# Sequence DFT with rows paired to their mirror, in batches 2 to 7 of a fused FNet and ELU kernel

## The chip, the cores and the metric

The kernel runs on one core of a Trainium2 chip, as one launch. The metric is device time in microseconds, the median of the runs. Five engines work side by side: TensorE (PE; matmuls and, overlapping them, weight loads), VectorE (DVE), ScalarE (ACT), GpSimd (POOL) and SyncE (SP), whose queue issues most of the DMA transfers. Each engine works through its instructions in the order in which they stand in the program, and waits where an operand isn't ready.

## The reference

```python
# x: (8, 3008, 256) float32, w_in: (256, 2048), w_out: (2048, 256)
X = np.fft.fft(x, axis=1)
X = np.fft.fft(X, axis=2)
y = X.real.astype(np.float32).reshape(8 * 3008, 256)
h = y @ w_in
g = np.where(h > 0.0, h, np.exp(np.minimum(h, 0.0)) - 1.0)
out = (g @ w_out).astype(np.float32)
```

So each batch gets a DFT along its sequence of 3008 rows and one along its 256 channels, of which the real part is kept, and then a two-layer network with ELU is applied to every row.

## The kernel before

**Folding.** The channel DFT is folded into the first weight matrix (`Wc` for the cosine part, `Ws` for the sine part), so at run time only the sequence DFT is computed. The input is real, so output rows k and 3008 - k come from the same two numbers, the cosine part R and the sine part I: h for row k is P + Q, for row 3008 - k it is P - Q. Only 1504 columns a batch are therefore needed, 12032 in all, in 47 tiles of 256 columns.

**The sequence DFT of a batch.** Four quarters of x, loaded as `xl0` to `xl3` (two of them backwards, by gathers with row tables `ix` from GpSimd's queue, L181; two forwards from SP, L197 and L198), are added and subtracted on GpSimd (`fold_x`, L527) to four sets of rows: even and odd in the channel direction (E for R, O for I), and for even and odd k (`kodd` 0 and 1). Each set has 6 blocks of 128 rows. A DFT unit (`Dft`, one for each of R and I and each `kodd`) has two halves, one for even and one for odd rows of the sequence. Each half is three matmuls against columns of a matrix `MC` (L430, in `dft_mms`); `dft_parts` gives block, first column, width and place in the PSUM bank. The even half is then unfolded: a copy on ScalarE (`anti`) and a sum and a difference on VectorE (L436) give `es`. The odd half is joined with it by `plus` and `minus`, one sum and one difference on VectorE (L436), into a ring of 2048 columns in SBUF (`Rr` for R, `Ir` for I), forwards and backwards. Where a run crosses the end of the ring, it is cut in two.

**The steps.** The rest is a sequence of 376 steps, eight for each tile of 256 columns, each for two blocks of 128 of d_ff. A step's matmuls: P (`H<-Rr,Wc`), Q (`H<-Ir,Ws`) and, from step 16 on, seven products against the second weight matrix in a form with 7 products in place of 8 (`mm_X1`, `mm_X2`, `mm_X3`, into `pA` to `pD`), which belong to the step before last. Between P and Q VectorE makes E (L839), which reads P and must be done before Q adds to the same bank. VectorE then makes the difference for row 3008 - k (L853) and both ELUs (L869), with ScalarE's `Relu` and `Exp` (L442). GpSimd makes four sums of G for the seven products (`sum_1`, `sum_3`, `sum_2`, `sum_4`, L439). At the end of a tile VectorE combines the four accumulators (u, v) and transposes them (L1017, L1038) into `ot`, of which there are two, and SP stores `ot`. In the first step of a tile, number 0, `mm_X3` is put off by most of a step, so that step number 2 has two matmuls fewer and number 3 two more.

**The order.** The order is written out by hand: `at(t, fn)` puts each piece of work at a time in units of the step period, and at the end all pieces are issued in the order of these times. Instructions of PE, DVE, ACT and POOL are pinned to this order; most DMAs of SP are placed by the framework. A batch b of 1 to 7 is computed while the tiles of batch b - 1 run: with s0 = 47 (b - 1) its loads stand from step s0 - 8 on, its folds from s0 - 1 to s0 + 38, and its four DFT units (R and I of kodd 0, then R and I of kodd 1) have their even halves at the ends of steps s0 + 28, 34, 38 and 42 and their odd halves two steps later. The unfold, and plus and minus, stand in the following step on VectorE, after E. In this text "step 2" and the like is the step's number within its tile of eight; since 47 is one short of a multiple of 8, it moves by one from batch to batch.

In the last batch one backward row does not exist, so a special table column is used for one gather and a plain transfer from GpSimd's queue (L192) puts the right row over it.

Of the kernel before, what the change touches and what calls it, by code (L numbers as in the profile page):

```python
# [9 lines left out]
FP = mybir.dt.float32  # L10
BF = mybir.dt.bfloat16
U32 = mybir.dt.uint32
# [15 lines left out]
NH = 189  # L28
BE = 4 * NH
BW = BE + 3 * NE  # L30
GW = 7 * TW
PERIOD = 4.8


def _dft_consts():

    p = np.arange(128)[:, None]
    out = np.zeros((128, 4, BW), np.float64)
    for ri in range(2):
        fn = np.cos if ri == 0 else np.sin
        for kodd in range(2):
            mat = out[:, 2 * ri + kodd]
            n, h = (NO, NO // 2) if kodd else (NE, NH)

            def block(m, n):  # L50
                k = 2 * np.arange(n)[None, :] + kodd
                s = 4 * p + m if m < 4 else 508 + 2 * p + m
                w = np.where(s == 0, 0.5, 1.0) * (s <= RUN)
                w = np.where(s == RUN, 0.5 if ri == kodd else 0.0, w)
                return s, w * fn(2.0 * np.pi * ((s * k) % SEQ) / SEQ)

            for m in (0, 2, 4):
                s, v = block(m, h)
                anti = (s % 4 == 2) != ri
                if not kodd:  # L60
                    v[:, h - 1] *= ~anti[:, 0]
                if m < 4:
                    c = 0 if m == 2 * ri else h
                    mat[:, c : c + h] = v
                else:
                    mat[:, 2 * h : 3 * h] = v * ~anti
                    mat[:, 3 * h : 4 * h] = v * anti
            for t in range(3):
                mat[:, BE + t * NE : BE + t * NE + n] = block(2 * t + 1, n)[1]
    return out.reshape(128, -1).astype(np.float32)  # L70


def _chan_consts():
# [33 lines left out]
def kernel(  # L107
# [11 lines left out]
    n_tiles = (n_cols + TW - 1) // TW  # L119

    MC_dr = nc.inline_tensor(_dft_consts(), name="dft_mats")
    CC_dr = nc.inline_tensor(_chan_consts(), name="chan_mats")
    PK_dr = nc.inline_tensor(_pick_consts(), name="pick_mats")

# [14 lines left out]
    def xrows(b, row, step, n, rows=6):  # L139

        return bass.AP(
            tensor=xt,
            offset=x.offset + (b * SEQ + row) * ND,
            ap=[[step * ND, n], [1, rows * ND]],
        )


    xflat = x.rearrange("b s d -> (b s) d")
    ix = cpool.tile([128, 3], I32, tag="ix")

    def row_tables():

# [17 lines left out]
    def load_x(b):  # L170

        L = [
            spool.tile([128, 6 * ND], FP, tag=f"xl{j}", bufs=1, name=f"xl{j}")
            for j in range(4)
        ]

        def back(j, few):
            cols = slice(0, 2 * ND) if few else slice(2 * ND, 6 * ND)
            c = 1 if few else 2 if j == 1 and b == NB - 1 else 0
            pin(  # L180
                nc.gpsimd.indirect_dma_start(  # L181
                    out=L[j][:, cols],
                    out_offset=None,
                    in_=xflat,
                    in_offset=bass.IndirectOffsetOnAxis(
                        ap=ix[:, c : c + 1].bitcast(U32), axis=0
                    ),
                    element_offset=(b * SEQ + (HALF if j == 1 else 0)) * ND,
                )
            )  # L190
            if b == NB - 1 and j == 1 and not few:
                nc.gpsimd.dma_start(  # L192
                    out=L[1][0:1, 2 * ND : 5 * ND], in_=xrows(b, SEQ - 3, 1, 1, 3)
                )

        def ahead(j, row):
            nc.sync.dma_start(out=L[j][:, 0 : 4 * ND], in_=xrows(b, row, 4, 128, 4))  # L197
            nc.sync.dma_start(  # L198
                out=L[j][:, 4 * ND :], in_=xrows(b, row + 512, 2, 128, 2)
            )  # L200

        loads = [lambda n=n: back(2 - n // 2, n % 2) for n in range(4)]
        return L, loads + [lambda: ahead(3, HALF), lambda: ahead(0, 0)]


    CC = cpool.tile([128, 384], FP, tag="CC")
# [191 lines left out]
    def load_mats(ri, kodd, cuts=()):  # L398
        n = (2 * ri + kodd) * BW
        ends = (0, *cuts, BW)  # L400
        for a, z in zip(ends, ends[1:]):
            nc.sync.dma_start(
                out=MC[ri, kodd][:, a:z], in_=MC_dr.ap()[:, n + a : n + z]
            )

    warm = cpool.tile([128, 1], FP, tag="warm")
    nc.vector.memset(warm, 0.0)
    Rr = cpool.tile([128, RING], FP, tag="Rr")
# [32 lines left out]
    def act(o, i, func=AF.Copy, **kw):  # L441
        pin(nc.scalar.activation(out=o, in_=i, func=func, **kw))  # L442
# [75 lines left out]
        gtt(W[3], W[1], b21, ALU.add)  # L518


    def fold_x(L, engine_of, cuts_of):

        ops = {}

        def op(key, o, a, b, f):
            tt = lambda o, a, b, f: pin(
                engine_of(key).tensor_tensor(out=o, in0=a, in1=b, op=f)  # L527
            )
            cuts = cuts_of(key, o.shape[1])
            for i in range(len(cuts) - 1):  # L530
                c = slice(cuts[i], cuts[i + 1])
                ops[key, i] = lambda c=c: tt(o[:, c], a[:, c], b[:, c], f)

        E, O = [], []
        for j in range(4):
            e = spool.tile([128, 6 * 128], FP, tag=f"e{j}", bufs=1, name=f"e{j}")
            o = spool.tile([128, 6 * 128], FP, tag=f"o{j}", bufs=1, name=f"o{j}")
            ev, ov = (
                t.rearrange("p (m o d) -> p m o d", o=2, d=64) for t in (e, o)
            )  # L540
            src = L[j].rearrange("p (m d) -> p m d", d=ND)
            if j in (1, 2):
                src = src[:, ::-1]

            lo, hi = (
                t.rearrange("p m (d o) -> p m o d", o=2)
                for t in (src[:, :, 1:129], src[:, :, 255:127:-1])
            )
            op(f"e{j}", ev, lo[:, :, ::-1], hi[:, :, ::-1], ALU.add)
            ops[f"c{j}", 0] = lambda e=ev[:, :, 0, 63:64], s=src[:, :, 0:1], j=j: (  # L550
                act(e, s)
                if engine_of("c") is nc.vector and j != 1
                else pin(engine_of("c").tensor_copy(out=e, in_=s))
            )
            op(f"o{j}", ov, lo, hi, ALU.subtract)
            E.append(e)
            O.append(o)
        ops["x1", 0] = lambda: act(L[1][0:1, 5 * ND :], L[0][0:1, 0:ND])
        op("E0", E[0], E[0], E[1], ALU.add)
        op("E2", E[2], E[2], E[3], ALU.add)  # L560
        op("EO0", E[1], E[0], E[2], ALU.add)
        op("EO1", E[3], E[0], E[2], ALU.subtract)
        op("O0", O[0], O[0], O[1], ALU.subtract)
        op("O2", O[2], O[2], O[3], ALU.subtract)
        op("EO2", O[1], O[0], O[2], ALU.subtract)
        op("EO3", O[3], O[0], O[2], ALU.add)
        return [E[1], E[3], O[1], O[3]], ops

    FOLDS = (
        "e0 c0 e3 c3 e2 c2 x1 e1 c1 E0 E2 EO0 o0 o3 o2 o1 O0 O2 EO2 EO1 EO3".split()  # L570
    )

    def fold_first(L):
# [57 lines left out]
    class Dft:  # L631
# [42 lines left out]
        def half(self):  # L674

            if self.ri == 0 and not self.kodd:
                R4b = R4[:, self.b : self.b + 1]
                vtt(R4b, self.es[:, 0:1], self.odd[:, 0:1], ALU.subtract)


    def load_ext(j, s0, s1):
        if j == 0 and s0 == 0:
# [495 lines left out]
        w2_chunks[5].load()  # L1178

    def open_x(b):  # L1180
        state["L"], state["loads"] = load_x(b)

    def begin_x_even():
        state["x_even"] = Dft(0, 0, 0, fold_first(L_first), ring=Rb, first=True)
# [219 lines left out]
    def at_dft(step, gap, b, ri, kodd, stat):  # L1404
        box = []

        def d():
            if not box:
                box.append(Dft(ri, b, kodd, stat()))
            return box[0]  # L1410

        at_half(step, d, 0, 0)
        at_half(step + gap, d, 1, b * HALF + (kodd + 1) * RUN)

    def begin_folds(b):
        state["EO"], state["ops"] = fold_x(
            state["L"], lambda key: nc.gpsimd, lambda key, n: (0, n // 2, n)
        )

    steps_b = HALF * 8 // TW  # L1420
# [20 lines left out]
    at(35 * T + 4.76, lambda: ext_side(3))  # L1441
    at(36 * T + 0.2, lambda: ext_unfold(1, vtt))
    at(36 * T + 1.5, lambda: ext_rows(1, vtt))
    fold_keys = [(k, p) for k in FOLDS for p in range(2 if k[0] not in "cx" else 1)]
    n_big = sum(k[0] not in "cx" for k, _ in fold_keys)
    for b in range(1, NB):
        s0 = (b - 1) * steps_b
        late = 2 if b == 1 else 0
        l0, gap = (s0 - 8, 1) if b > 1 else (3.2, 0.5)
        if b > 1:  # L1450
            at(l0 * T + 0.1, lambda b=b: open_x(b))
        for n in range(6):
            t = l0 + gap * n if n < 4 else l0
            if b > 1:
                at(t * T + 0.2, lambda n=n: state["loads"][n]())
        first = (6, 7, 7, 8, 9, 9, 10, 10, 12, 15)

        def fold_slot(n):
            if b > 1:
                return s0 - 1 + 39 * n // n_big  # L1460
            return first[n] if n < len(first) else 17 + n - len(first)
# [3 lines left out]
        for key in fold_keys:  # L1465
            slot = fold_slot(n)
            at(
                slot * T + (3.5 if slot < 16 else 1.3),
                lambda key=key: state["ops"][key](),
            )  # L1470
            n += key[0][0] not in "cx"
        for n, (ri, kodd) in enumerate(((0, 0), (1, 0), (0, 1), (1, 1))):
            at_dft(
                s0 + (28, 34 + late, 38 + late, 42 + late)[n], 2, b, ri, kodd,
# [54 lines left out]
```

## Time and profile before

| | us |
|---|---|
| median of 3 runs | 1945.42 |
| lowest and highest | 1945.23, 1945.55 |
| span of the profiled execution | 1943.2 |
| steps 16 to 375, from first P to last P | 121.63 to 1925.40 |

| busy, from the page and its groups | us | count |
|---|---|---|
| GpSimd, sums of G (L439) | 1036.8 | 1440 |
| VectorE, E (L839) | 327.7 | 752 |
| VectorE, difference and both ELUs | 256.8, 255.8, 256.7 | 376 each |
| GpSimd, first folds of x (L527, 128x384) | 66.6 and 66.0 | 56 and 56 |
| GpSimd, folds of folds | 56.2 and 56.1 | 56 and 56 |
| GpSimd, gathers (L181) | 32.5 | 32 |

A row of the groups gives line, engine and operation, then output and inputs by their names in the program, shapes, count, busy time and the mean of one, and the idle time just ahead of it. In the timelines a line holds start, duration over all the merged instructions, engine, line, operation, names, shape and count, and in brackets the idle time of the engine just ahead of it and who ended it. The recorded duration of a matmul reaches beyond the start of the next one, since matmuls are pipelined.

### The profile page before, as it was taken

How to read it: one execution, taken by the hardware profiler on the slowest of the kernel's cores; microseconds unless marked ns; L12 is line 12 of the kernel's file. 1: busy time of each engine (PE TensorE's matmuls, PEld its weight loads, DVE VectorE, ACT ScalarE, POOL GpSimd, SP SyncE). 2: the span in 40 equal slices, each digit the busy share in tenths (PEclk: the TensorE clock that was granted, in tenths of full speed). 3: DMA queues.
4: the chain of work that ended last, by engine and by line, in shares of the span. 5: the costliest groups of instructions: out<-in, count | busy, mean ns of one | idle time of the engine just before them, and what ended most of it. 6: DMA issues, size and time to landing. Idle time of an engine off the chain costs nothing.

```text
span 1943.2 us, 26993 instructions
## 1 busy us (share of the span) xinstructions
PE 1933.4 (99%) x8912; PEld 1653.4 (85%) x8912; DVE 1293.2 (67%) x2398; ACT 865.6 (45%) x1671; POOL 1377.6 (71%) x1816
## 2 busy tenths in 40 slices
PE   9999999999999999999999999999999999999999
PEld 6788788888888888888888888888888888888887
DVE  8866666666666666666667666676666766667666
ACT  5644434443444444444444443444434444344443
POOL 4788758876677767787677876777767776556655
PEclk9999999999999999999999999999999999999999
DMA  8145111101112020020210202012020110100101
GB/s 333 44 35 52 34 44 19 49 15 33 33 20 49 12 50 21 18 50 11 54 23 13 52 8 58 12 20 60 7 52 11 20 23 14 17 12 11 23 11 23
DMA packets 263291, 70.25 MB, mean 36 GB/s; under 512 B 248607, under 2 KB 249523, under 8 KB 263153
## 3 DMA queue, kind: packets, MB, share of 16 engines
q1 hardware_dynamic: 257360, 55.69, 14.8%
q0 software_dynamic: 3616, 12.59, 2.1%
q8 instruction: 70, 1.15, 0.2%
q14 instruction: 69, 0.56, 0.1%
q10 hardware_dynamic: 2176, 0.26, 0.1%
HBM read 43.66 MB, written 24.80 MB: 35 GB/s over the span
## 4 chain that ended last, share of the span: by engine, by line
PE 94%; DVE 2%; POOL 2%; ACT 1%; DMA 1%; issue 1%; DVEq 0%; POOLq 0%
PE H L430 38%; PE pB L430 16%; PE pC L430 16%; PE pD L430 16%; PE pA L430 8%; DMA xl<-in_x_dram,ix 1%; POOL WT L439 1%; POOL G L439 1%; DVE G L869 0%; DVE E L839 0%; DVE e L527 0%; POOL w L439 0%; DVE v L436 0%; ACT G L442 0%; DVE pow L310 0%
## 5 line engine op out<-in xcount | busy, mean ns | idle before, releaser
L439 POOL TENSOR_TENSOR G<-G 128x256 f32<-128x256 f32 x1440 | 1036.8, 730 | 508.5 <-DVE G L869 338.6
L839 DVE SCALAR_TENSOR_TENSOR E<-Rb,wex,H 128x256 f32<-128x256 f32 x752 | 327.7, 477 | 544.7 <-PE H L430 541.1
L442 ACT ACTIVATE G<-H 128x512 f32<-128x512 f32 x376 | 224.6, 597 | 960.1 <-DVE G L853 955.4
L430 PE MATMUL H<-Ir,Ws 128*128 128x256 f32 x1504 | 386.9, 380 | 2.0 <-DVE E L839 2.0
L430 PE MATMUL H<-Rr,Wc 128*128 128x256 f32 x1504 | 387.0, 380 | 0.8 <-DVE Ir L436 0.8
L430 PE MATMUL pC<-G,WT 128*128 128x256 f32 x1440 | 369.5, 379 | 0.0
L430 PEld LDWEIGHTS H<-Rr,Wc 128*128 128x128 f32 x1504 | 284.6, 190 | 56.0 <-issue 2.2
L430 PEld LDWEIGHTS H<-Ir,Ws 128*128 128x128 f32 x1504 | 278.8, 189 | 49.6 <-DVE E L839 4.3
L430 PEld LDWEIGHTS pC<-G,WT 128*128 128x128 f32 x1440 | 273.6, 190 | 37.2
L853 DVE SCALAR_TENSOR_TENSOR G<-E,H 128x512 f32<-128x512 f32 x376 | 256.8, 683 | 44.2 <-POOL G L439 5.0
L869 DVE SCALAR_TENSOR_TENSOR G<-G,H 128x512 f32<-128x512 f32 x376 | 255.8, 680 | 43.0 <-ACT G L442 43.0
L869 DVE SCALAR_TENSOR_TENSOR G<-M,G 128x512 f32<-128x512 f32 x376 | 256.7, 683 | 0.4 <-ACT M L442 0.4
L442 ACT ACTIVATE G<-G 128x512 f32<-128x512 f32 x376 | 233.2, 620 | 0.0
L430 PE MATMUL pD<-G,w 128*128 128x256 f32 x784 | 229.4, 379 | 0.5 <-POOL G L439 0.5
L430 PE MATMUL pA<-G,w 128*128 128x256 f32 x784 | 229.3, 379 | 0.0
L430 PE MATMUL pB<-G,w 128*128 128x256 f32 x784 | 229.3, 379 | 0.0
L442 ACT ACTIVATE M<-G 128x512 f32<-128x512 f32 x376 | 224.0, 596 | 3.1 <-DVE G L853 3.1
L442 ACT ACTIVATE M<-M 128x512 f32<-128x512 f32 x376 | 221.0, 588 | 0.1
L430 PE MATMUL pB<-G,WT 128*128 128x256 f32 x720 | 214.8, 380 | 0.3
L430 PE MATMUL pD<-G,WT 128*128 128x256 f32 x720 | 214.1, 379 | 0.0
L430 PEld LDWEIGHTS pD<-G,w 128*128 128x128 f32 x784 | 148.9, 190 | 21.1 <-POOL G L439 0.9
L430 PEld LDWEIGHTS pA<-G,w 128*128 128x128 f32 x784 | 149.0, 190 | 20.5
(148 smaller groups left out, 1408.2 us busy)
## 6 DMA issues: line engine op xcount, KB each, us to landing
out_dram<-ot SPq DMA_DIRECT2D x496, 32.0 KB
xl<-in_x_dram SPq DMA_DIRECT2D x16, 512.0 KB
xl<-in_x_dram SPq DMA_DIRECT2D x16, 256.0 KB
out_dram<-ot SPq DMA_DIRECT2D x256, 2.0 KB
Rb<-r SPq DMA_DIRECT2D x10, 376.0 KB
raw<-in_moe_w_in_dram SPq DMA_DIRECT2D x7, 512.0 KB
MC<-dft_mats SPq DMA_DIRECT2D x3, 943.5 KB
raw<-in_moe_w_out_dram SPq DMA_DIRECT2D x4, 512.0 KB
```

The lines of the kernel that those rows point to most:

```text
L430: nc.tensor.matmul(out_, lhsT=lhsT, rhs=rhs, start=start, stop=stop, skip_group_check=True)
L439: pin(nc.gpsimd.tensor_tensor(out=o, in0=a, in1=b, op=op))
L442: pin(nc.scalar.activation(out=o, in_=i, func=func, **kw))
L839: nc.vector.scalar_tensor_tensor(out=S.E[:, c], in0=Rb[:, cols(i)], scalar=wex[:, f : f + 1], in1=S.H[:, c], op0=ALU.mult, op1=ALU.add,)
L853: nc.vector.scalar_tensor_tensor(out=two(S.G[:, 0:512])[:, :, ::-1], in0=two(S.E), scalar=2.0, in1=two(S.H), op0=ALU.mult, op1=ALU.subtract,)
L869: nc.vector.scalar_tensor_tensor(out=o, in0=e, scalar=-1.0, in1=h, op0=ALU.add, op1=ALU.max)
```

## The change

For batches 2 to 7 the rows of a quarter are no longer put in 6 blocks by their distance modulo 4 or 2, but in three pairs of blocks in which each row of a multiple of 8 has its mirror at a distance 4 modulo 8 in the same place (`_row_pairs`). Blocks 0, 2 and 4 hold even rows, 1, 3 and 5 odd ones. The even half then splits once more: parts a (rows of multiples of 8), b (4 modulo 8) and c (2 modulo 4) are computed for a quarter or half of the k alone and unfolded twice, near (a and b) and far (with c). For `kodd` 0 the odd half splits too: sums and differences of blocks 1 and 3 (S and D) are formed on GpSimd and multiplied with half the columns each. In `kodd` 1 the odd half keeps its width.

The new matrices (1417 columns for kodd 0, 1786 for kodd 1) are loaded into the buffers of the old ones at steps 52, 55, 58 and 61. x is loaded by 11 transfers from SP and 6 gathers a batch, where there were 4 and 4; the table gets four more columns, made at steps 34 to 37, and the plain transfer of the last batch goes. Batches 0 and 1 keep the old form.

```diff
+NA = (95, 94)
+NC = (189, 188)
+MW = (1417, 1786)
...
-    ix = cpool.tile([128, 3], I32, tag="ix")
+    ix = cpool.tile([128, 7], I32, tag="ix")
...
-            if b == NB - 1 and j == 1 and not few:
-                nc.gpsimd.dma_start(
-                    out=L[1][0:1, 2 * ND : 5 * ND], in_=xrows(b, SEQ - 3, 1, 1, 3)
-                )
...
+    def mirror_table(c):
...
+            pin(
+                nc.gpsimd.iota(
+                    ix[first : first + n, c + 3 : c + 4],
+                    pattern=[[0, 1]],
+                    base=base,
+                    channel_multiplier=-8,
+                )
+            )
+        if c == 1:
+            pin(
+                nc.vector.tensor_scalar(
+                    out=ix[:, 4:5], in0=ix[:, 4:5], scalar1=0x3FF, scalar2=None,
+                    op0=ALU.bitwise_and,
+                )
+            )
+
+    def load_mirror(b):
...
+        def gather(j, pair):
...
+                nc.gpsimd.indirect_dma_start(
+                    out=L[j][:, 2 * block * ND : (2 * block + 2) * ND],
...
+        def ahead(j):
+            pairs = L[j].rearrange("p (m c) -> p m c", c=2 * ND)[:, 0::2]
+            for p, q, row, gap in ((0, 64, 0, 4), (64, 96, 512, -254), (96, 128, 500, 14)):
+                nc.sync.dma_start(
...
+        def back(j):
...
+            cuts = (0, 80, 94, 128) if j == 1 else (0, 96, 128)
+            for p, q in zip(cuts, cuts[1:]):
+                s = 750 - 8 * p if p < 94 else 1018 - 8 * p
+                nc.sync.dma_start(
...
+        loads = [
+            lambda j=j, pair=pair: gather(j, pair)
+            for j, pair in ((3, 1), (2, 0), (2, 2), (0, 1), (1, 0), (1, 2))
+        ]
+        loads += [
+            lambda: ahead(3), lambda: back(2), lambda: ahead(0), lambda: back(1)
+        ]
...
+    def load_mirror_mats(ri, kodd):
+        t = cpool.tile([128, BW], FP, tag=f"MC{ri}{kodd}", name=f"MM{ri}{kodd}")
+        MM[ri, kodd] = t
+        n = MOFF[2 * ri + kodd]
+        nc.sync.dma_start(out=t[:, 0 : MW[kodd]], in_=MM_dr.ap()[:, n : n + MW[kodd]])
...
+        for n, t in ((0, E[1]), (2, O[1])):
+            d = spool.tile([128, 380], FP, tag="side", bufs=2, name=f"sd{n}")
+            sd.append(d)
+            for m, f in ((0, ALU.add), (1, ALU.subtract)):
+                op(
+                    f"{'SD'[m]}{n}",
+                    d[:, 128 * m : 128 * m + 128],
+                    t[:, 128:256],
+                    t[:, 384:512],
+                    f,
+                )
...
+    MIRROR_FOLDS = (
+        "e0 c0 e3 c3 e2 c2 x1 e1 c1 E0 E2 EO0 S0 D0 o0 o3 o2 o1 O0 O2 EO2 S2 D2 EO1 EO3".split()
+    )
...
+    def mirror_parts(ri, kodd, par):
+        na, nc_ = NA[kodd], NC[kodd]
+        if not par:
+            return [
+                (0, 0, 2 * na, 0),
+                (2, 2 * na, nc_, 2 * na),
+                (4, 2 * na + nc_, na + nc_, na),
+            ]
+        z = 3 * na + 2 * nc_
+        if kodd:
+            return [(2 * t + 1, z + t * NO, NO, 0) for t in range(3)]
+        n = (188, 189) if ri else (189, 188)
+        return [
+            (6, z, n[0], 189 if ri else 0),
+            (7, z + n[0], n[1], 0 if ri else 189),
+            (5, z + NE, NE, 0),
+        ]
...
+    def unfold_near(even, near, ab, ri, kodd, M, tt):
+        na, nc_ = NA[kodd], NC[kodd]
+        a, b, ab = even[0:M, 0:na], near[0:M, 0:na], ab[0:M]
+        tt(ab[:, 0:na], a, b, ALU.add)
+        p, q = (b, a) if ri else (a, b)
+        tt(ab[:, steps_of(nc_ - 1, 94, -1)], p[:, 0:94], q[:, 0:94], ALU.subtract)
+
+    def unfold_far(es, even, ab, ri, kodd, M, tt):
+        na, nc_ = NA[kodd], NC[kodd]
+        n = NO if kodd else NE
+        c, ab = even[0:M, 2 * na : 2 * na + nc_], ab[0:M]
+        tt(es[0:M, 0:nc_], ab[:, 0:nc_], c, ALU.add)
+        p, q = (c, ab) if ri else (ab, c)
+        tt(es[0:M, steps_of(n - 1, 188, -1)], p[:, 0:188], q[:, 0:188], ALU.subtract)
+
+    def join(es, odd, kodd, to, tt, ri=0, part=None):
...
+            if kodd:
+                put(up, base if up else top, NO, 1 if up else -1, run(es, 0, 1), run(odd, 0, 1))
+                continue
+            for h in range(2):
+                first = h if up or h else 2
+                n = (189, 188)[h] if up else (187, 188)[h]
+                put(
+                    up,
+                    base + first if up else top - first + 1,
+                    n,
+                    2 if up else -2,
+                    run(es, first, 2),
+                    run(odd, 189 * h + first // 2, 1),
+                )
...
-                box.append(Dft(ri, b, kodd, stat()))
+                box.append((Mirror if b > 1 else Dft)(ri, b, kodd, stat()))
...
+    for n in range(4):
+        at((34 + n) * T + 4.3, lambda n=n: mirror_table(n))
+    for n in range(4):
+        at((52 + 3 * n) * T, lambda n=n: load_mirror_mats(n % 2, n // 2))
...
-        for n in range(6):
-            t = l0 + gap * n if n < 4 else l0
+        for n in range(10):
+            t = l0 + n if n < 6 else l0
```

`Mirror` is a `Dft` whose `mms` takes these parts from the new matrices, whose `unfold` is near and then far, and whose `plus` and `minus` call `join`; `S` and `D` stand in the folds without a step of their own.

## The prediction

> **What bounds the kernel now.** I read the page first (busy shares, then the chain that ended last), then who waited for whom, then the timelines of single steps. Page:
>
> ```profile
> span 1943.2 us, 26993 instructions
> PE 1933.4 (99%) x8912; PEld 1653.4 (85%) x8912; DVE 1293.2 (67%) x2398; ACT 865.6 (45%) x1671; POOL 1377.6 (71%) x1816
> PEclk9999999999999999999999999999999999999999
> PE 94%; DVE 2%; POOL 2%; ACT 1%; DMA 1%; issue 1%; DVEq 0%; POOLq 0%
> ```
>
> TensorE is never throttled and is 94% of the chain. But its busy share counts modelled ends, so I take starts from the timeline of TensorE, one step of 256 columns against two blocks of d_ff:
>
> ```profile
> 1000.36 1.03 PE L430 MATMUL H<-Rr,Wc 128*128 128x256 f32 x4
> 1001.22 0.59 PE L430 MATMUL pA<-G,w 128*128 128x256 f32 x2
> ...
> 1005.11 0.81 PE L430 MATMUL H<-Rr,Wc 128*128 128x256 f32 x3
> ...
> 1434.34 2.06 PE L430 MATMUL H<-MC,e 128*128 128x376 f32 x6
> 1436.24 0.59 PE L430 MATMUL H<-Rr,Wc 128*128 128x256 f32 x2
> ```
>
> Each matmul leaves two records. Four records take 1001.22 - 1000.36 = 0.86 us, 0.2155 us each; a step of 11 matmuls takes 1005.11 - 1000.36 = 4.75 us = 22 x 0.216. Six records of 376 columns (an odd DFT half, three matmuls) take 1.90 us, 0.317 each. Both fit columns/1.2 + 2.5 ns per record, so a matmul costs 1.667 ns a column and nothing else. Adding up what every start after 70 us lies behind this rule gives 9.3 us, about 7 of them in 17 places between 100 and 1935 us. So a column taken from TensorE is time gained, unless another engine then makes it wait. Where it waits today:
>
> ```profile
> 946.30 2.35 POOL L439 TENSOR_TENSOR G<-G 128x256 f32<-128x256 f32 x3 [0.40 <-DVE G L869]
> 947.23 0.59 PE L430 MATMUL pB<-G,w 128*128 128x256 f32 x2
> 947.90 0.70 PE L430 MATMUL pB<-G,WT 128*128 128x256 f32 x2
> 1439.90 0.55 POOL L192 DMA_DIRECT2D xl<-in_x_dram  x1 [3.69 <-DMA xl<-in_x_dram,ix]
> 1441.26 0.70 PE L430 MATMUL pD<-G,w 128*128 128x256 f32 x2 [0.55 <-POOL G L439]
> 504.56 0.60 DVE L436 TENSOR_TENSOR bs<-H,anti 127x188 f32<-127x188 f32 x2
> 505.08 0.68 DVE L869 SCALAR_TENSOR_TENSOR G<-G,H 128x512 f32<-128x512 f32 x1
> ```
>
> The first three lines: the step numbered 2 in its tile of eight is only 3.88 us long on TensorE (two of its matmuls come a step later), and a DFT half in front of it gives VectorE more to do; its ELU ends late, GpSimd's second sum with it, and TensorE starts 0.24 us late, then 0.10 more at the next pair. The fourth and fifth: in the last batch GpSimd waits 3.69 us for a gather before a plain transfer into the same row; TensorE loses 0.71 + 0.10 us. The last two: the two unfold operations of an even half hold VectorE 505.08 - 504.56 = 0.52 us.
>
> **What the skill says.** TensorE: Matmul & The Clock Gate, Back-to-back issue gap, gives N/2.4 + 2.5 ns; the trace's fp32 records have the same fixed 2.5 ns and half that rate. Perfetto Trace Analysis, Identifying the Most-Contended Engine, says that matmul busy share misleads: hence the starts. VectorE: DVE Perf Modes, The TRN2 errata, gives (N+151)/0.96 ns for an fp32 tensor_tensor: 353 ns at 188, the rows show 343; at 94 it would be 255, an estimate. Rules for kernel authors there says to minimize operation count; here independent operations follow at about 60 ns + N/0.96 (0.26 us for 188, 0.46 for 376), so four small ones cost more than two large.
>
> **The change, part by part.** *Fewer columns.* The order of instructions shows six matmuls a DFT unit as before, with other widths. kodd 0: even 189+189+378 becomes 190+189+284, odd 3 x 377 becomes 189+188+377: 1887 columns become 1417. kodd 1: even 188+188+376 becomes 188+188+282, odd stays: 1880 become 1786. Two units of each a batch: 2 x (470 + 94) = 1128 columns, at 1.667 ns 1.88 us; six batches, 11.3 us, all on the path. Narrow matmuls already run at 159 ns a record for 188 columns although a weight load's record lasts 190, so I count none as bound by its load; if those that become narrow in the odd halves were, 12 halves x 4 records x 30 ns = 1.4 us would go.
>
> *The plain transfer of the last batch* goes, replaced by a row of the index table: 0.8 us gained.
>
> *VectorE, even halves (24).* Two operations become four, of 95, 94, 189, 188. The second pair reads what the first wrote; from the combination of a tile, where v follows u after 0.79 us instead of 0.60, I take 0.19 us for such a dependence. Chain: 0.16, then 0.16 + 0.19, then 2 x 0.26 = 1.02 us instead of 0.52: 0.5 more. Between DFT halves VectorE idles 0.9 to 1.6 us ahead of E, so 16 of 24 cost nothing. Eight do. Steps shift by one in eight from batch to batch (47 steps each), and the unfold of four even halves falls into a step 2 (at 458, 502, 898, 1425 us). There the second sum ends 0.27 us before its matmul starts and 0.05 is the least seen, so 0.5 leaves 0.28 + 0.10 for the restart, four times: 1.5 us. Four fall into a step 1 (at 694, 738, 1135, 1662), where the tile's combination runs right before the E of step 2: that E starts 0.31 late, 0.16 of it is slack, 0.15 + 0.10, four times: 1.0 us.
>
> *VectorE, odd halves of kodd 0 (12).* Each run over the ring splits into even and odd places: two operations become four, three become six where the ring wraps, 0.12 to 0.18 us more. Four fall where VectorE has no idle time left and TensorE waits already, at 941 and 1382 us (step 2), 1178 and 1619 (step 1): 0.6 us in all. The splits step by 8 bytes. The fold's stride-2 reads on VectorE cost 955 ns for 768 elements against 950 for unit stride, so I take nothing; no row shows a stride-2 write. At half rate each such operation would add 0.2 us, 0.8 a half; at the four places, 3.2 us. That is the upper end.
>
> *GpSimd.* Two sums and two differences of 128 columns a batch, 0.46 us each (the WT rows), 0.92 at steps 16 and 33 of a batch. GpSimd is idle 0.4 to 0.6 us a step there, and the sums end 0.73 us or more before use: the rest, 0.3 to 0.5, is hidden. Uncovered: up to 0.4 each, 12 times. Gathers: six of about 1.0 us instead of four, one a step at steps 39 to 44, where no folds stand; each delays the fourth sum alone, which has 2.05 us or more in hand at the two new places. Nine iotas of 0.12 us once, at 217 to 240 us: they delay a sum by 0.25 where TensorE waits 1.38 us for E anyway. The one VectorE operation on the table waits for the second pair, until about 225.3, inside its 0.54 us of idling for ScalarE: nothing.
>
> *SP and DMA.* Eleven loads of x a batch instead of four, of the same bytes; four matrix loads of 0.73 to 0.91 MB in place of none. Each matrix load waits on SP for TensorE's last read of the old matrix, at about 209, 243, 264 and 287 us; behind them stand stores whose data came at 222.7, 269.9 and 311.0. Free. The new loads of xl2 and xl1 wait on SP for folds (until step 22 to 24), in some batches ahead of a tile's 16 stores, which then go up to 9 us later; the output tile has two buffers of 38 us. Hidden.
>
> **Sum.** 11.3 + 0.8 - 1.5 - 1.0 - 0.6 = 9.0 us. Against the profiled 1943.2 us span that is 1934.2; the runs' median is 2.2 us above the span, so 1936.4.
>
> **Rivals.** *A, the sum:* 1936.4. For it: the rule of columns is exact, and waits of this very kind are in the trace. *B, VectorE's additions vanish too:* 1945.4 - 12.1 = 1933.3. For it: no even half reaches TensorE today. Against: 0.27 us of slack is less than 0.5. *C, strided operations at half rate:* 3.2 us more, 1939.6. For it: none is in the trace; against: strided reads are free. *D, slower: SP's queue.* The x loads that wait on SP for folds hold back stores and the spreading of r into Rb behind them. Up to 9 us is covered by the second output buffer; from about 30 us on, the transpose on VectorE waits and TensorE with it. If each of six batches lost 2.5 us on top of A, 1936.4 + 15 = 1951.4. Against: SP issues 16 stores in 8.5 us of every 38. That the columns do not shrink is ruled out by the widths in the instruction order.
>
> **Chances.** A 0.62, B 0.14, C 0.16, D 0.05, the rest (a wait nobody named, between the values) 0.03. A's own range is 1935 to 1938.5. The stated range 1933.0 to 1940.5 takes in B, C and the weight loads' 1.4. A measurement of this kernel tells 0.2%, 3.9 us, from no change, so faster means below 1941.5: A, B, most of C: 0.90; same 0.05; slower 0.05.
>
> **What would show it.** Right: DFT halves of 1.11 and 1.27 us where 1.27 and 1.90 stood; no plain transfer wait near 1430 us; short waits for GpSimd's sum or for E at the eight and four places named; everywhere else 4.75 us a step. Wrong: a strided operation on VectorE near 0.55 us instead of 0.35 (C); stores or Rb transfers late and VectorE idle before its transposes (D); or a step longer than 4.75 us away from DFT halves.

## The result and the profile after

The median is 1936.13 us (5 runs, 1935.43 to 1937.37) against 1945.23 beside it: a ratio of 0.9953, 95% interval 0.9941 to 0.9966, so 9.1 us less. 1936.4 had been predicted. The profiled execution, the slowest of the five, has a span of 1934.6 us; the run with the median time has 1934.1, and 1934.2 had been predicted. The page, in the same lines as before:

```profile
span 1934.6 us, 27221 instructions
PE 1923.9 (99%) x8912; PEld 1651.4 (85%) x8912; DVE 1305.2 (67%) x2475; ACT 864.3 (45%) x1672; POOL 1398.6 (72%) x1860
PEclk9999999999999999999999999999999999999999
PE 94%; DVE 3%; POOL 2%; ACT 1%; issue 1%; DMA 0%; DVEq 0%; POOLq 0%
```

The number of matmul records is the same, 8912, and their busy time is 9.5 us less; VectorE has 12.0 us more work and GpSimd 21.0 more. VectorE's share of the chain is 3% where it was 2%. The timeline of TensorE over an even and an odd half of kodd 0 in batch 2 (start, duration of the merged records, count) shows the new widths as time:

```profile
425.82 1.29 PE L567 MATMUL H<-MM,e 128*128 128x190 f32 x6
426.94 0.59 PE L567 MATMUL H<-Rr,Wc 128*128 128x256 f32 x2
...
436.44 0.80 PE L567 MATMUL H<-MM,sd 128*128 128x189 f32 x4
437.07 0.80 PE L567 MATMUL H<-MM,e 128*128 128x377 f32 x2
437.71 0.59 PE L567 MATMUL H<-Rr,Wc 128*128 128x256 f32 x2
```

From start to start the even half takes 426.94 - 425.82 = 1.12 us, the odd one 437.71 - 436.44 = 1.27, of which the four narrow records 0.63, 0.158 each. Both are the predicted lengths. So VectorE's share is where to look for what was given back. Its timeline in a step 2 and the step 3 behind it, in the last batch, then GpSimd's and TensorE's of the same stretch:

```profile
1420.43 0.41 DVE L573 TENSOR_TENSOR ab<-H,near 128x94 f32<-128x94 f32 x2
1420.88 0.61 DVE L573 TENSOR_TENSOR bs<-ab,H 128x188 f32<-128x188 f32 x2
1421.41 0.68 DVE L1160 SCALAR_TENSOR_TENSOR G<-G,H 128x512 f32<-128x512 f32 x1
...
1422.61 0.68 DVE L1160 SCALAR_TENSOR_TENSOR G<-M,G 128x512 f32<-128x512 f32 x1
...
1423.37 1.53 POOL L576 TENSOR_TENSOR G<-G 128x256 f32<-128x256 f32 x2 [0.40 <-DVE G L1160]
...
1424.29 0.59 PE L567 MATMUL pB<-G,w 128*128 128x256 f32 x2
...
1424.95 0.70 PE L567 MATMUL pB<-G,WT 128*128 128x256 f32 x2
...
1425.49 1.03 PE L567 MATMUL H<-Ir,Ws 128*128 128x256 f32 x4
```

The unfold holds VectorE for 1421.41 - 1420.43 = 0.98 us (0.52 before). Its ELUs follow without a gap, GpSimd idles 0.40 us for the second one, its second sum ends at 1423.37 + 1.53 = 1424.90, and only then the pair of matmuls that reads it starts: 1424.95 - 1424.29 = 0.66 us after its predecessor instead of 0.43, and the next 0.54 instead of 0.43. That is a wait of 0.23 and then 0.10 more at the next pair of matmuls, which this text calls the restart. The same matmuls before the change, with 0.44 and 0.43 from pair to pair:

```profile
1430.88 0.59 PE L430 MATMUL pB<-G,w 128*128 128x256 f32 x2
1431.32 0.59 PE L430 MATMUL pB<-G,WT 128*128 128x256 f32 x2
1431.75 1.03 PE L430 MATMUL H<-Ir,Ws 128*128 128x256 f32 x4
```

There an even half in step 2 had cost nothing.

Worked out in this way from the starts of all matmuls, the waits (with their restarts) between 400 and 1700 us are 3.7 us in place of 2.1. Of GpSimd's wait near 1430 us in the last batch this is left:

```profile
1429.09 0.96 POOL L293 DMA_INDIRECT xl<-in_x_dram,ix  x1
1430.07 0.73 POOL L576 TENSOR_TENSOR G<-G 128x256 f32<-128x256 f32 x1
1433.64 2.23 POOL L576 TENSOR_TENSOR G<-G 128x256 f32<-128x256 f32 x3 [2.83 <-DVE G L1160]
```

A sum follows the gather at once; the idle 2.83 us after it is for VectorE's next result and keeps nobody waiting. TensorE's wait of 0.71 + 0.10 us is gone.

### The profile page after: what moved, and what is told of

It reads as the page before. It is cut to its first block, busy times and chain, and to the rows that moved or that the text cites. A ratio compares the mean times of both kernels' runs of the same rounds, so it can differ in the third digit from the quotient of the medians.

```text
span 1934.6 us, 27221 instructions
## 1 busy us (share of the span) xinstructions
PE 1923.9 (99%) x8912; PEld 1651.4 (85%) x8912; DVE 1305.2 (67%) x2475; ACT 864.3 (45%) x1672; POOL 1398.6 (72%) x1860
## 4 chain that ended last, share of the span: by engine, by line
PE 94%; DVE 3%; POOL 2%; ACT 1%; issue 1%; DMA 0%; DVEq 0%; POOLq 0%
PE H L567 37%; PE pB L567 16%; PE pC L567 16%; PE pD L567 16%; PE pA L567 8%; POOL WT L576 1%; POOL G L576 1%; DVE G L1160 0%; DVE E L1130 0%; DMA xl<-in_x_dram,ix 0%; DVE v L573 0%; DVE u L573 0%; DVE e L664 0%; POOL w L576 0%; DVE G L1144 0%
## 5 line engine op out<-in xcount | busy, mean ns | idle before, releaser
L567 PEld LDWEIGHTS pB<-G,w 128*128 128x128 f32 x784 | 148.9, 190 | 20.3
```

Source lines behind the costliest of these rows:

```text
L567: nc.tensor.matmul(out_, lhsT=lhsT, rhs=rhs, start=start, stop=stop, skip_group_check=True)
```

## The experiments

Two sets of four, each set on one chip beside the kernel before (1945.47 and 1945.22 us). The changed kernel was not run again beside them; where a run is compared with its 1936.13 us, the comparison leans on the kernel before, which took 1945.23 us beside that. The theory throughout is the prediction's: columns are paid at 1.667 ns each, and what VectorE gets in addition is paid only where it has no slack, in the steps 1 and 2 of a tile.

**The columns alone.** In the kernel before, for batches 2 to 7:

```diff
+    def narrow_parts(ri, kodd, par):
...
+        if par:
+            z = [BE + t * NE for t in range(3)]
+            return [(1, z[0], 189, 0), (3, z[1], 188, 189), (5, z[2], 377, 0)]
+        h, w = (188, 282) if kodd else (189, 284)
+        return [(2 * ri, 0, h, 0), (2 - 2 * ri, h, h, h), (4, 2 * h, w, 2 * h - w)]
...
```

`dft_mms` takes these parts where b > 1; odd halves of kodd 1 keep theirs.

> The kernel before, with nothing changed but the widths of the DFT matmuls of batches 2 to 7, which are cut to those of the changed kernel (third even part 284 or 282 columns, odd parts of kodd 0 189 + 188 + 377); part of the columns is left out, so the output is another. If a column is 1.667 ns and nothing else depends on it, 6 x 1128 columns are 11.3 us: 1945.2 - 11.3 = 1933.9, with the same waits of TensorE as before (947.9, 992.5, 1388.8, 1441.3 us less the shift). If narrow matmuls are bound by their weight loads, up to 1.4 us less: 1935.3. If a step that ends sooner only makes TensorE wait for E or for a sum of G, new waits near the odd halves and a gain well below 10 us.

Measured: 1934.09 us (1933.44 to 1936.36), ratio 0.9941 (0.9927 to 0.9954), 11.4 us less. Narrow matmuls are not held by their weight loads. The waits are those of before but one: the plain transfer's wait grew from 0.71 to 1.00, as TensorE arrives there 8.9 us sooner and the transfer, which waits for a gather, only 8.65. On GpSimd, then TensorE, in this run:

```profile
1431.25 0.55 POOL L192 DMA_DIRECT2D xl<-in_x_dram  x1 [3.98 <-DMA xl<-in_x_dram,ix]
```

```profile
1431.18 0.59 PE L430 MATMUL pD<-G,WT 128*128 128x256 f32 x2
1432.61 0.70 PE L430 MATMUL pD<-G,w 128*128 128x256 f32 x2 [0.83 <-POOL G L439]
```

**The second unfold left out.** In the changed kernel:

```diff
-            M, h = self.M, NA[self.kodd]
+            M, h = self.M, (self.n + 1) // 2
...
-            ab = spool.tile([128, NH], FP, tag="ab", bufs=2, name="ab")
-            unfold_near(self.even, self.near, ab, self.ri, self.kodd, self.M, vtt)
-            unfold_far(self.es, self.even, ab, self.ri, self.kodd, self.M, vtt)
+            unfold(self.es, self.even, self.near, self.M, self.n, vtt)
```

The first two lines give ScalarE's copy the width that it had before the change.

> The changed kernel with the even half unfolded once, by two operations of 188 or 189 columns as before, in place of four; the second unfold is left out, so the output is another. If VectorE's two added operations make the eight waits at even halves (464, 508, 902, 1425 us of 0.33 each; 699, 743, 1138, 1660 of 0.10 to 0.13), these go: 1.8 us, 1936.1 - 1.8 = 1934.3, and the waits at odd halves (945, 989, 1180, 1383, 1618) stay. If GpSimd's new sums and differences or the loads make them, they stay: 1936.1.

Measured: 1935.08 us (1933.79 to 1936.03), ratio 0.9942 (0.9929 to 0.9956), 0.8 us above what was expected, with runs that scatter by 2.2 us. The time alone doesn't decide; the trace does. TensorE at the place that was shown above (2.1 us sooner here):

```profile
1422.34 0.59 PE L567 MATMUL pB<-G,w 128*128 128x256 f32 x2
1422.77 0.59 PE L567 MATMUL pB<-G,WT 128*128 128x256 f32 x2
1423.20 1.03 PE L567 MATMUL H<-Ir,Ws 128*128 128x256 f32 x4
```

0.43 from pair to pair: no wait. All eight waits at even halves are gone, and those at odd halves keep the sizes that they have in the changed kernel: 1.91 us of waits between 400 and 1700 in place of 3.70. So neither GpSimd's new work nor the loads make these waits. In the profiled execution 5.4 us pass between the last matmul's start and the end of the span, 3.5 in the changed kernel's; the last stores fall there, and this time scatters. The run shows that the two added operations make the waits; how much of their 0.46 us is work and how much is the second pair waiting for the first, it does not separate.

**The joins in one piece.** In the changed kernel, kodd 0 is joined in the form that kodd 1 has already:

```diff
-            if kodd:
-                put(up, base if up else top, NO, 1 if up else -1, run(es, 0, 1), run(odd, 0, 1))
+            if True:
+                o, n = (0, NO if kodd else NE) if up else (1 - kodd, NO if kodd else NE - 2)
+                put(up, base if up else top, n, 1 if up else -1, run(es, o, 1), run(odd, o, 1))
```

> The changed kernel with the odd halves of kodd 0 joined by one sum and one difference over the whole run with unit step, as before, in place of two each with a step of two; the order of the columns within a half is not restored, so the output is another. If the split of these operations is the cause, the waits at 945 and 1383 fall from 0.48 to 0.34 us, those at 1180 and 1618 from 0.32 and 0.25 to 0.13: 0.6 us, 1935.5. If the step of two is free the split operations already last what unit-step ones of their width do (0.345 us), and the gain is that of fewer operations alone. If the waits come from elsewhere: 1936.1.

Measured: 1935.62 us, ratio 0.9947 (0.9934 to 0.9961); 0.5 less than the changed kernel, whose own five runs lie 1.9 us apart, so the time alone would show nothing. The trace is finer: the waits at the four places are 0.34, 0.33, 0.13 and 0.13 as before the change, and those at even halves stay at 0.33 and 0.10 to 0.13; one of 0.10 is new, at 1060. The four places together are 0.57 us. That the step of two is free shows in the changed kernel itself, in VectorE's groups by shape (count, busy us, mean ns): the strided join, which reads and writes SBUF with a step of two, and an unfold with unit step, of the same width.

```profile
L573 DVE TENSOR_TENSOR Rr<-bs,H 128x188 f32<-128x188 f32 x10 | 3.4, 345 | 0.0
...
L573 DVE TENSOR_TENSOR bs<-H,anti 128x188 f32<-128x188 f32 x3 | 1.0, 347 | 0.0
```

**The transfer alone.** In the kernel before:

```diff
-            if b == NB - 1 and j == 1 and not few:
-                nc.gpsimd.dma_start(
-                    out=L[1][0:1, 2 * ND : 5 * ND], in_=xrows(b, SEQ - 3, 1, 1, 3)
-                )
```

> The kernel before without the plain transfer of the last batch; one row of x is therefore a wrong one. Theory: GpSimd no longer waits 3.69 us near 1436 us, the wait of TensorE at 1441.3 us (0.71 + 0.10) goes and nothing else moves: 1945.2 - 0.8 = 1944.4. Rival: the gather that it waited for holds the next fold back instead, and some of it stays: 1945.2.

Measured: 1944.77 us, 0.7 less, ratio 0.9995 (0.9987 to 1.0004), which alone would not tell it from nothing. In the trace the wait of 0.81 us is gone and no other has changed by more than 0.03:

```profile
1435.37 0.97 POOL L181 DMA_INDIRECT xl<-in_x_dram,ix  x1
1436.36 0.73 POOL L434 TENSOR_TENSOR G<-G 128x256 f32<-128x256 f32 x1
```

**A second dose.** The changed kernel with two more additions after each unfold:

```diff
+            sp = spool.tile([128, NH], FP, tag="ab", bufs=2, name="sp")
+            n = NC[self.kodd]
+            for m in range(2):
+                vtt(sp[0 : self.M, 0:n], self.es[0 : self.M, 0:n], ab[0 : self.M, 0:n], ALU.add)
```

> The changed kernel with two further additions of 189 or 188 columns on VectorE after each even half's unfold, some 0.6 to 0.7 us more in each of 24 places. Theory of slack: at the four even halves in a step 2 and the four in a step 1 the slack is used up already, so each loses the full amount, 5 us in all; at the other sixteen VectorE still has 0.4 to 1.1 us of idle time ahead of E, so they lose nothing or up to 0.2: 1936.1 + 4.5 to 7 = 1940.6 to 1943. If VectorE's work costs the same wherever it stands: 24 x 0.65 = 15.6, 1951.7. If the waits do not come from VectorE: 1936.1.

Measured: 1943.98 us, 7.9 more than the changed kernel, a microsecond above the expected span of values and far from both rivals. VectorE in the place shown above:

```profile
1426.98 0.74 DVE L573 TENSOR_TENSOR sp<-bs,ab 128x188 f32<-128x188 f32 x2
1427.64 0.68 DVE L1164 SCALAR_TENSOR_TENSOR G<-G,H 128x512 f32<-128x512 f32 x1
```

The dose is 1427.64 - 1426.98 = 0.66 us. TensorE there:

```profile
1427.71 1.03 PE L567 MATMUL H<-Rr,Wc 128*128 128x256 f32 x4
1428.97 0.70 PE L567 MATMUL pD<-G,WT 128*128 128x256 f32 x2 [0.23 <-DVE v L573]
...
1430.37 0.59 PE L567 MATMUL pB<-G,w 128*128 128x256 f32 x2
1431.18 0.70 PE L567 MATMUL pB<-G,WT 128*128 128x256 f32 x2 [0.22 <-POOL G L576]
```

There are two waits now, first for v (0.40 + 0.10), then for the sum (0.38 + 0.11): 0.99 where 0.33 was, which is the dose to the hundredth. The places in a step 1 went from 0.10 to 0.13 up to 0.79: again the dose. Of the other sixteen even halves 14 lost 0.21 each and two nothing. 8 x 0.66 + 14 x 0.21 = 8.2 us, which is what the waits grew by. So where the slack is used up a microsecond on VectorE costs TensorE a microsecond; elsewhere the first 0.5 was free, and of a further 0.66 a third showed. The expectation had named 0 to 0.2 us for those sixteen, and its range for the total, up to 7, was too narrow.

**The halves moved.** The changed kernel, for batches 2 to 7:

```diff
+        def free(s):
+            return s + {1: -1, 2: 1}.get((s + 1) % 8, 0) if b > 1 else s
+
-        at_half(step, d, 0, 0)
-        at_half(step + gap, d, 1, b * HALF + (kodd + 1) * RUN)
+        at_half(free(step), d, 0, 0)
+        at_half(free(step + gap), d, 1, b * HALF + (kodd + 1) * RUN)
```

> The changed kernel with those 14 halves of batches 2 to 7 whose unfold or join falls in a step 1 or 2 of a tile moved by one step (from 1 back to 0, from 2 on to 3). If it is the place in the tile that lacks slack, all of the waits between 460 and 1665 us go, 3.7 us, and none comes: 1936.1 - 3.7 = 1932.4. If the wait belongs to the half wherever it stands (a bank, a fold, a load that is late), they move with it: 1936.1.

Measured: 1931.78 us (1931.60 to 1932.08), ratio 0.9932 (0.9918 to 0.9945). Between 230 and 1700 us there is not one wait of 0.03 us or more left. The time fell by 4.4 us and not by 3.7; in the profiled executions 0.8 us of it lies in the first 124 us, ahead of anything that was edited. The same matmuls again:

```profile
1420.36 0.59 PE L567 MATMUL pB<-G,w 128*128 128x256 f32 x2
1420.79 0.59 PE L567 MATMUL pB<-G,WT 128*128 128x256 f32 x2
1421.22 1.03 PE L567 MATMUL H<-Ir,Ws 128*128 128x256 f32 x4
```

So it is the place in the tile, not the half. GpSimd's new sums and differences, the gathers and the loads are all still there, and no wait follows them.

**The table and the extra rows moved as well.** On top of that:

```diff
-        at((34 + n) * T + 4.3, lambda n=n: mirror_table(n))
+        at((34 + n) * T + 2.5, lambda n=n: mirror_table(n))
...
-    at(36 * T + 0.2, lambda: ext_unfold(1, vtt))
+    at(36 * T + 1.4, lambda: ext_unfold(1, vtt))
```

> As the run with moved halves, and the iotas of the new table stand behind the folds and ahead of the first sum of a step instead of ahead of the third, and the unfold of the extra rows at 226 us stands after E instead of ahead of it. Theory: the wait for GpSimd's sum at 226.6 us falls from 0.64 to what it was before (0.22), and that for E at 228.4 (1.26 + 0.10) goes; 1.8 us in all, of which some may come back as a wait for a later E, 0.5: 1932.4 - 1.3 to 1.8 = 1930.6 to 1931.1. If E there waits for the transfer or the copies instead of the unfold: 1932.

Measured: 1930.15 us (1930.07 to 1930.31), ratio 0.9923 (0.9909 to 0.9936), the fastest here. The wait for E at 228 us (1.26 + 0.10) is gone, that for the sum fell from 0.64 to 0.26, and 0.05 + 0.10 is new a step later. The wait for E stood in the kernel before too, so this gain is not the change's.

**The kernel before with its halves moved.** The edit of `at_dft` under "The halves moved", with `b > 1`, on the kernel before.

> The kernel before with the same move of the halves of batches 2 to 7. Its waits at odd halves (948, 992, 1185, 1229, 1389, 1626 us) are 0.34, 0.27, 0.13, 0.17, 0.34 and 0.13, 1.4 us: 1945.5 - 1.4 = 1944.1. So if the change's waits differ from these in their size alone, the change is worth 1944.1 - 1932.4 = 11.7 with the halves moved, its columns and the transfer and nothing else. If the moved halves meet other waits: 1945.5 or more.

Measured: 1943.47 us, ratio 0.9991 (0.9983 to 1.0000), 1.75 less. All the waits at odd halves went, and the plain transfer's fell from 0.81 to 0.34, which had not been expected and stays unexplained. With the halves moved in both kernels the change is worth 1943.47 - 1931.78 = 11.7 us by the medians and 1941.2 - 1929.8 = 11.4 by the profiled spans: about the columns' 11.3 and what was left of the transfer's wait, less 0.3 for the iotas (see below).

## Why the prediction was right

| step | predicted, us | measured, us | by |
|---|---|---|---|
| columns | -11.3 | -11.4 | columns alone |
| plain transfer | -0.8 | -0.7; 0.81 in the trace | transfer alone |
| even halves in a step 2, four | +1.5 | +1.33 (4 x 0.33) | second unfold left out, dose |
| even halves in a step 1, four | +1.0 | +0.46 | the same |
| odd halves, four places | +0.6 | +0.57 | joins in one piece |
| table, loads, GpSimd, SP | 0 | +0.3 | trace |
| waits in the first 70 us | 0 | +0.4 | trace |

The first two rows are differences of medians, the others sums from the traces. With 0.81 for the transfer they come to 9.1 us. That this lies within 0.1 us of the 9.0 predicted is in part luck: the even halves were reckoned 0.7 us too dear, and the last two rows, 0.7 us together, stand in no term of the prediction. The last row is scatter. The two profiled executions differ by 8.6 us, as the columns are 11.3 there, and small waits that stand in no row and a later end add some 0.3 us; and from run to run the time of the changed kernel lies 1.7 to 2.8 us above its span, where the prediction took 2.2.

**Columns.** The rule of 1.667 ns a column held down to 188 columns, and all of it was on the path. The reserve for weight loads wasn't needed. The prediction's "and nothing else" passes over the 2.5 ns a record of its own rule; they drop out, since a unit has six matmuls before and after.

**Even halves.** The four places in a step 2 are the ones named (458, 502, 898 and 1425 us, and TensorE waits at 464.5, 508.3, 902.6 and 1425.0), each with 0.23 + 0.10 where 0.28 + 0.10 was reckoned: the unfold takes 0.98 - 0.52 = 0.46 us more and not 0.5, and 0.46 less the 0.22 of slack is 0.24. In a step 1 the places were right and the size was off by half. At 698 us the first ELU of the step, v and E on VectorE, then TensorE with the matmul that waits for E:

```profile
695.32 0.68 DVE L1160 SCALAR_TENSOR_TENSOR G<-G,H 128x512 f32<-128x512 f32 x1
...
697.90 0.69 DVE L573 TENSOR_TENSOR v<-u,pC 128x512 f32<-128x512 f32 x1
698.50 0.87 DVE L1130 SCALAR_TENSOR_TENSOR E<-Rb,wex,H 128x256 f32<-128x256 f32 x2
```

```profile
697.24 1.03 PE L567 MATMUL H<-Rr,Wc 128*128 128x256 f32 x4
...
699.42 1.13 PE L567 MATMUL H<-Ir,Ws 128*128 128x256 f32 x4
```

The same place before the change:

```profile
696.35 0.69 DVE L869 SCALAR_TENSOR_TENSOR G<-G,H 128x512 f32<-128x512 f32 x1
...
698.93 0.69 DVE L436 TENSOR_TENSOR v<-u,pC 128x512 f32<-128x512 f32 x1
699.73 0.87 DVE L839 SCALAR_TENSOR_TENSOR E<-Rb,wex,H 128x256 f32<-128x256 f32 x2
```

```profile
698.67 1.03 PE L430 MATMUL H<-Rr,Wc 128*128 128x256 f32 x4
```

E starts 698.50 - 697.24 = 1.26 us after its P, 1.06 before the change (699.73 - 698.67). It is late by 0.20 us and not by the 0.31 that the prediction took; with 0.16 of slack that leaves 0.04 and the restart. The term that was too large is the one of the lateness that passes through the ELUs and the combination to E. The first ELU is 0.40 us late against P (1.92 us ahead of it in place of 2.32), and from v to E 0.60 us pass in place of 0.80: that takes up the other 0.20.

**Odd halves.** Their four places and the sum came out; the upper end, for strided operations at half rate (rival C), is excluded by the 345 ns, against the 550 or so reckoned for half rate. Rival B, all additions hidden, is excluded by the waits in the steps 2.

**GpSimd.** A pair of S and D takes 0.86 us, where 0.92 was reckoned, and delays a fold and then the next sums; no wait of TensorE follows. At 365 us:

```profile
365.01 0.86 POOL L664 TENSOR_TENSOR sd<-e 128x128 f32<-128x128 f32 x2
...
365.83 1.18 POOL L664 TENSOR_TENSOR o<-xl 128x384 f32<-128x384 f32 x1
...
366.96 1.42 POOL L576 TENSOR_TENSOR G<-G 128x256 f32<-128x256 f32 x2
```

**SP (rival D).** The longest time between a transpose's end and the first of its stores is 4.1 us (2.9 before); up to 9 had been reckoned, and either is covered by the second output buffer. VectorE's idle time before its transposes is nil, and between 400 and 1925 us the profile shows no wait of VectorE for a transfer, those into Rb included, so nothing of this reached anyone.

**The iotas** (GpSimd's operations that write the new columns of the index table) are where a step failed. They were to delay a sum under the cover of a wait of TensorE for E. But the sum's matmul stands ahead of that wait, and was waiting already. On GpSimd, then TensorE:

```profile
224.08 1.41 POOL L576 TENSOR_TENSOR G<-G 128x256 f32<-128x256 f32 x2 [1.21 <-PE pD L567]
225.45 0.32 POOL L266 IOTA ix<- 128x1 int32 x2
225.85 1.53 POOL L576 TENSOR_TENSOR G<-G 128x256 f32<-128x256 f32 x2
```

```profile
226.63 0.70 PE L567 MATMUL pB<-G,WT 128*128 128x256 f32 x2 [0.48 <-POOL G L576]
228.42 0.92 PE L567 MATMUL H<-Ir,Ws 128*128 128x256 f32 x3 [1.09 <-DVE E L1130]
```

Two iotas stand between the sums, the wait of 0.22 became 0.64, and that for E became only 0.12 shorter: 0.3 us. The run with the table moved moved both the iotas and the extra rows' unfold; that the smaller wait for the sum is the iotas' doing alone was not tried.

The beginnings of the ten profiled executions here differ although every edit acts later: TensorE's first wait for a sum of G falls between 133.6 and 134.4 us. In the changed kernel's a wait of 0.56 us stood at 13.8 us that the others do not show. That is scatter, as is 3.3 to 5.4 us after the last matmul. These make most of the differences of half a microsecond between what the waits and what the medians say.

## What to carry to other kernels

Where TensorE runs without gaps, work taken from it is time (here 11.4 us measured for 11.3 taken), and the question is only who pays for it: count the added operations of another engine at each place separately, as the same half microsecond was free in sixteen places, 0.33 us in four and 0.12 in four. When a piece of work drifts through a periodic pattern (47 steps against tiles of 8), list where each instance lands and move those few that land on the tight steps by one; here that took away 3.7 us of waits, of which 1.4 had stood in the kernel before, with no work removed. A wait that comes later on the same engine is no cover for one that comes before it.

## What was not expected of the hardware

The three VectorE operations on 8 rows at 221 us (`rx`, both operands in SBUF) took 2.45 us instead of 1.77, with the same shapes. What differs is which GpSimd operations run beside them: two iotas stood ahead of two sums of G, which with the fold behind them came 0.3 us later against the step, so that both long operations, 1.11 and 1.34 us, met a GpSimd operation, where before only the first did (1.25) and the second took 0.53. With the iotas moved away (the run with the table moved) they took 1.25 and 0.53 again. The Trainium skill, SBUF — State Buffer, SBUF: two separate sides, says that a VectorE operation with two SBUF inputs and a GpSimd operation that reads SBUF take turns at a shared pair of ports, each for a whole instruction; the trace agrees, with 0.53 us alone and up to 1.34 beside another. GpSimd's fold in the same stretch took 1.31 us instead of 1.00. The two operations just ahead (`bs<-side`, two SBUF inputs) went the other way: the second took 0.34 us beside an iota, which has no input, and 0.88 before the change, beside a sum of G. The unfold and join operations of the change each have one operand in PSUM, and their group means stay at 344 to 354 ns for 188 and 189 columns.
